# Eight weight pairs by seven products, and an order written by hand for all eight batches

## The chip, the cores and the metric

The kernel runs on one core of one Trainium2 chip. The metric is the device time of one execution in microseconds: 708.32 us is the median of the 3 runs before the change (706.35 to 708.89).

## The reference

Two softmax attentions per head, then a two-layer block on all 4608 tokens. Batch 8, 8 heads, 576 tokens, head width 64, 32 packed rows; model width 512, inner width 2048.

```python
def sm_attn(qq, kk, vv):
    a = softmax(qq @ kk.T / 8)          # over the last axis
    return a @ vv
p_packed = sm_attn(p, k, v)             # 32 rows per head
x = sm_attn(q, p_packed, p_packed)      # 576 rows per head, heads side by side: 4608 x 512
h = x @ w_in                            # 512 -> 2048
g = h * clip(h + 3, 0, 6) / 6
out = g @ w_out                         # 2048 -> 512
```

q, k, v and p are float32; w_in and w_out come as float64 and are narrowed on the chip.

## The kernel before, in words

**Precision.** The large products are made from float32r parts: each operand is split into a high and a low part, and each product is three matmuls (high·high, high·low, low·high; `product`, from L967).

**First layer.** The values of the second attention are folded into w_in: `u_m` multiplies the packed rows of a batch with each quarter of w_in into `m_hi`, `m_lo` (matmuls at L350), so that `first_product` (L929) makes one of 16 blocks f of h, transposed, from the attention weights `a_hi`, `a_lo` by six matmuls, three for each of two groups of heads. A block covers 256 or 320 tokens of one half of a batch, c = 0 or 1; `ps_h` holds two blocks.

**Gate.** `gate_into` writes min(relu(h+3), 6)·h with ScalarE (L940) and VectorE (L941). A block's last 64 columns of the wide half are edge rows, put aside in `bnd` by GpSimd (L965), and two batches' edges make a block of 128 rows.

**Second layer.** For a single block f, `gated` splits 256 columns into parts (ScalarE L946, VectorE L947), and `single_product` adds 2 x 3 matmuls of 512 columns (L969) to two banks. Two blocks 2i, 2i+1 can be taken as a pair: the 2x2 product of token halves and weight quarters is made by **seven** products of 256 columns, 21 matmuls (`pair_product`), from sums of the gated values (VectorE L1241, L1249, L1254) that GpSimd splits (L947, in `parted`). The weight side, T1 to T4, is made once, in batch 1, by `combine` (POOL L1072, VectorE from L1083 on); T3 takes the place of a quarter of w_out, and T1, T2, T4 lie in one of four slots. Batch 1's second half uses four pairs (`FIRST_PAIRS`), each half of batches 2 to 7 six pairs (`PAIRS = 6`) and four single blocks after them. Pairs 4 and 5 share slots with 0 and 1: `t_kept` in DRAM holds them, and `fetch_t` (L1105) brings two back per half.

**End of a half.** After the last pair `pair_product` reads the four banks A to D: one ScalarE copy of C (L1134), a GpSimd add (L1136) and three VectorE adds of D (L1139). The four single blocks then go on into A and B, two VectorE adds (L1153) finish the rows, and SyncE stores them (L1156). The edges of batches 4 to 7 are made by pairs in `moe_edges`, those of 2 and 3 inside batch 3, those of 0 and 1 by single products in batch 1.

**Attention of the next batch** runs beside the second layer: scores in two rounds of 288 columns (`scores`, `both_halves`), whose PSUM banks are `ps_a` and, where both go at once, two accumulator banks.

**Batch 0** has its own path: `first_attention` with transposed loads, `s2` whose scores lie head by token and are turned by VectorE (L852), scaled on GpSimd (L866) and turned back (L868), then `first_moe` over whole blocks (L607).

**Order.** Batch 0 is in the order of `PLAN`, one word for each step of a generator (611 words). It fixes PE, ACT, DVE, POOL and SP, SP being the queue on which nearly all transfers are asked for. Its loads go k, rest of k, two blocks of w_out (`lo0 lo2`), v of the first four heads, q, then w_in among the rest. From batch 1 on, no order is written: `fill` calls parts of the next attention at fixed steps (`STAGES`, `LATE`, `TURN`, `FETCHES`), and the framework's scheduler puts them among the loop's own instructions.

Of the kernel before, what the change touches and what calls it, by code (L numbers as in the profile page):

```python
# [25 lines left out]
TURN = (
    (5, 5, 6, 6, 7, 7, 7), (7, 8, 8, 9, 9, 9, 10), (10, 10, 11, 11, 12, 12, 12), (13, 13, 13, 14, 14, 15, 15),  # L30
    (27, 27, 28, 28, 28, 29, 29), (29, 29, 30, 30, 30, 31, 31),
)
# [2 lines left out]
PLAN = """
in in in in lo0 lo2 in in k0 in p li0 k1 in p k0 k2 k1 kr k2 in s0 kr b2 s0 b0 k3 s0 b2 li1 s0 warm b2 s0 in
k3 b2 in b0 s1 s0 li2 q1 b2 e0 q1 c0 s1 b2 e0 q0 c0 li3 s0 s1 v0 q0 s0 s1 s1 v0 b0 lp s1 b0 e1 a0 v0 c1 qr
v0 e1 c1 s1 a0 z0 qr b0 s1 a0 z0 b0 v1 a0 z0a a1 z0a upper a1 z0a lo1 q2 v1 li4 a1 q3 q2 z0a a1 v1 q3 v1 z0a  # L40
z1 z1 li7 a2 m0 z1a a2 m1 a2 z1a a2 lo3 a3 z1b z0a lk0 a3 z1b z1b z0a z1b z0a z1a z0a z1b lo5 z1a b1 li6 z1a
z1b m0 z1b b1 z1a z1a z1b z0a a4 z1a m0 li5 z1b z0a warm a3 z1b z0a m1 m0 z1b a7 lk2 z1a h0 m0 z1a m1 b1 a7
z1a b1 b3 h0 b3 lo4 b3 a3 warm r0 m1 a4 r0 b3 m2 lo8 tp h1 r0 m1 a7 y0 b1 h1 r0 m2 lo6 a4 x0 b1 r1 a4 x0 m2
m2 a6 r1 x0 a6 m2 h2 a7 tk0 r1 h2 y1 a5 lk3 r1 a5 x0 y1 a5 x1 r2 a6 a5 b5 x1 r2 b3 x1 tk2 r2 y0 h3 a6 b4 r2
lk1 h3 b4 b5 m4 x1 b3 r3 b4 li8 b5 m4 b4 li10 r3 x2 li9 m4 m4 x2 lo7 r3 m4 b5 below h4 b4 tk3 y3 b6 h4 b4 y3
lq1 y2 b6 x2 r3 b5 x2 b6 r4 tk1 x3 b6 b8 r4 x3 a8 b5 S a8 x3 a8 r4 y4 a8 S S S S x3 b8 y4 h5 a10 li11 r4 a10
lo9 h5 a10 a9 b8 lq3 x4 b8 r5 x4 b6 r5 S x4 y2 a10 r5 tq1 h6 lo10 b8 r5 lq2 h6 y5 a9 y5 S x4 a9 r6 b8 x5 a9
S b7 S x5 r6 a11 x5 li12 S a11 a11 h7 b6 r6 a11 S h7 r6 x5 b9 r7 li13 m8 S lv b7 b7 x6 r7 y6 b7 m8 x6 y7 r7
# [125 lines left out]

# [1338 lines left out]
```

## Time and profile before

| what | value |
|---|---|
| median of 3 runs | 708.32 us (706.35 to 708.89) |
| the profiled execution's own time | 709.52 us |
| its span, first to last instruction | 707.7 us |
| mean granted TensorE clock | 0.99 |
| PE, DVE, ACT, POOL busy | 97%, 77%, 61%, 47% of the span |
| moved by DMA | 111.15 MB, mean 157 GB/s |
| critical chain by engine | PE 82%, DVE 7%, DMA 5%, issue 2% |

The span leaves out what lies around the program, 1.8 us here. A PE shown as busy is one whose modelled matmuls overlap, so the pitch from one start to the next, not the duration, tells what a matmul costs in a row of them.

### The profile page before, as it was taken

What the parts mean: (1) busy time and instruction counts of PE and PEld (TensorE: products, weight loads), DVE (VectorE), ACT (ScalarE), POOL (GpSimd) and SP (SyncE); (2) the same over time, 40 slices, a digit from 0 to 9 for tenths busy, and PEclk for the clock granted to TensorE, in tenths of its full rate; (3) what the DMA queues carried; (4) which work ended last, traced back from release to release, by engine and by line L of the source; (5) the groups of instructions that cost most, each with busy time, mean ns of one, the idle gap of its engine ahead of it and who ended that gap; (6) DMA issues with size and microseconds to landing.
All of it is one profiled execution on the core that took longest, in us unless ns stands there. A gap on an engine that the chain in (4) does not pass through costs nothing.

```text
span 707.7 us, 16190 instructions
## 1 busy us (share of the span) xinstructions
PE 684.7 (97%) x5924; PEld 591.9 (84%) x5924; DVE 544.2 (77%) x1227; ACT 428.8 (61%) x1004; POOL 335.9 (47%) x515
## 2 busy tenths in 40 slices
PE   6599999999999999999999999999999999999997
PEld 4477877888879888899898888899888988899997
DVE  2897788788999759877788777877698778867754
ACT  5798876556566646565455655656475755565553
POOL 2475541113425456371272626474453646475552
PEclk9699999999999999999999999999999999999999
DMA  9989852955338655465554647375755644340330
GB/s 277 310 216 240 218 141 88 287 150 116 117 123 208 161 131 210 127 158 108 107 200 125 164 103 232 121 158 129 196 200 143 168 127 150 129 170 1 120 119 30
DMA packets 199679, 111.15 MB, mean 157 GB/s; under 512 B 173489, under 2 KB 185265, under 8 KB 195761
## 3 DMA queue, kind: packets, MB, share of 16 engines
q1 hardware_dynamic: 199056, 109.94, 55.8%
q8 instruction: 46, 0.75, 0.4%
q14 instruction: 33, 0.26, 0.1%
q10 hardware_dynamic: 544, 0.20, 0.1%
HBM read 92.27 MB, written 17.83 MB: 156 GB/s over the span
## 4 chain that ended last, share of the span: by engine, by line
PE 82%; DVE 7%; DMA 5%; issue 2%; SPq 1%; ACT 1%; POOL 1%; DVEq 0%; ACTq 0%; POOLq 0%
PE acc L969 48%; PE ps_hh L929 22%; PE ps L350 5%; PE ps_h L607 3%; DMA w_again<-w_kept 2%; PE ps L470 1%; SPq L294 1%; DMA room<-in_q_dram 1%; PE ps L440 1%; DMA wt<-t_kept 1%; DVE tr L555 1%; DMA p_nat<-in_p_dram 1%; DVE osb L1153 1%; PE ps L273 1%; DVE t L941 0%
## 5 line engine op out<-in xcount | busy, mean ns | idle before, releaser
L929 PE MATMUL ps_hh<-a_hi,m_hi 128*128 128x320 f32 (+1 forms) x448 | 133.5, 298 | 1.0 <-DVE t L941 0.9
L929 PE MATMUL ps_hh<-a_lo,m_hi 128*128 128x320 f32 (+1 forms) x448 | 133.0, 297 | 0.0
L929 PE MATMUL ps_hh<-a_hi,m_lo 128*128 128x320 f32 (+1 forms) x448 | 132.7, 296 | 0.0
L969 PE MATMUL acc<-wo_hi,g 128*128 128x512 f32 x304 | 109.0, 402 | 0.0
L940 ACT ACTIVATE t<-ps_hh,three 128x320 f32<-128x320 f32 (+1 forms) x148 | 73.5, 500 | 47.4 <-PE ps_hh L929 36.0
L941 DVE SCALAR_TENSOR_TENSOR t<-t,ps_hh 128x320 f32<-128x320 f32 (+1 forms) x148 | 65.7, 445 | 45.1 <-ACT t L940 44.4
L947 POOL TENSOR_TENSOR ge<-t,ge 128x256 fp32r<-128x256 f32 x76 | 60.3, 793 | 80.8 <-ACT ge L946 32.1
L929 PEld LDWEIGHTS ps_hh<-a_hi,m_hi 128*128 128x128 f32 x448 | 84.7, 189 | 7.7 <-DVE t L941 2.7
L929 PEld LDWEIGHTS ps_hh<-a_lo,m_hi 128*128 128x128 f32 x448 | 84.7, 189 | 4.8 <-issue 1.9
L929 PEld LDWEIGHTS ps_hh<-a_hi,m_lo 128*128 128x128 f32 x448 | 84.7, 189 | 1.7 <-issue 1.3
L965 POOL COPY bnd<-t 128x64 f32<-128x64 f32 x76 | 24.2, 318 | 120.0 <-DVE t L941 117.8
L969 PE MATMUL acc<-wt,ga 128*128 128x256 f32 x492 | 80.4, 284 | 0.3 <-ACT ga L946 0.2
L969 PE MATMUL acc<-wo_hi,ge 128*128 128x256 f32 x328 | 77.8, 285 | 0.0
L947 POOL TENSOR_TENSOR gf<-tb,gf 128x256 fp32r<-128x256 f32 x76 | 65.0, 855 | 17.5 <-ACT gf L946 14.9
L947 POOL TENSOR_TENSOR ga<-t,ga 128x256 fp32r<-128x256 f32 x76 | 60.8, 800 | 24.4 <-ACT ga L946 24.2
L969 PEld LDWEIGHTS acc<-wo_hi,g 128*128 128x128 f32 x304 | 56.1, 188 | 16.2 <-issue 3.0
L969 PEld LDWEIGHTS acc<-wt,ga 128*128 128x128 f32 x492 | 68.0, 190 | 1.2 <-issue 0.5
L969 PEld LDWEIGHTS acc<-wo_hi,ge 128*128 128x128 f32 x328 | 57.5, 190 | 7.0 <-issue 2.8
L969 PE MATMUL acc<-wo_lo,g 128*128 128x512 f32 x152 | 60.1, 395 | 0.0
L555 DVE STREAM_TRANSPOSE tr<-nat 128x576 f32<-128x576 f32 x56 | 42.4, 765 | 16.7 <-DMA nat<-in_q_dram 10.4
L940 ACT ACTIVATE tb<-ps_hh,three 128x256 f32<-128x256 f32 (+1 forms) x76 | 37.9, 499 | 23.0 <-PE ps_hh L929 18.6
L969 PE MATMUL acc<-wt,gf 128*128 128x256 f32 x246 | 50.1, 283 | 0.3 <-DMA wt<-t_kept 0.3
(234 smaller groups left out, 1780.5 us busy)
## 6 DMA issues: line engine op xcount, KB each, us to landing
w_again<-w_kept SPq DMA_DIRECT2D x24, 1024.0 KB, 4.8
wt<-t_kept SPq DMA_DIRECT2D x26, 768.0 KB, 5.2
out_dram<-osb SPq DMA_DIRECT2D x35, 256.0 KB, 2.4
nat<-in_k_dram SPq DMA_DIRECT2D x112, 72.0 KB, 3.2
nat<-in_q_dram SPq DMA_DIRECT2D x112, 72.0 KB, 2.7
raw_out<-in_moe_w_out_dram SPq DMA_DIRECT2D x10, 512.0 KB, 5.1
raw_in<-in_moe_w_in_dram SPq DMA_DIRECT2D x10, 512.0 KB, 5.6
w_kept<-w_in_sb SPq DMA_DIRECT2D x4, 1024.0 KB, 7.6
```

Of the source, the lines that this page charges most:

```text
L273: nc.tensor.matmul(banks[x][NPK * a:NPK * a + NPK, :n * P], state["pp"][half, NPAIR * x + a], cols[half, :, a], start=True, stop=True,)
L294: nc.sync.dma_start(out=t[r:r + 32], in_=src[b, 2 * a + h, :, 32 * c:32 * c + 32].rearrange("(t i) j -> i t j", i=32),)
L350: nc.tensor.matmul(pair[x][NPK * a:NPK * a + NPK, :n], rows[half, a], c, start=True, stop=True)
L440: nc.tensor.transpose(out=pair[x][:, c * P:(c + 1) * P], in_=e[x][:, c * P:(c + 1) * P], identity=ident)
L555: nc.vector.transpose(out=t, in_=state.pop(("nat", which, b, a)))
L607: nc.tensor.matmul(h[:, hf, :HS], mm[:, g, fs], aa[:, hf * HS:(hf + 1) * HS], start=(g == 0 and i == 0), stop=(g == NG - 1 and i == 2),)
L929: state["first"] = nc.tensor.matmul(h[:, :n], mm[:, g, fs], aa[:, t0:t0 + n], start=(g == 0 and i == 0), stop=(g == NG - 1 and i == 2),)
L940: state["relu"] = nc.scalar.activation(out=t[:, :n], in_=h, func=AF.Relu, bias=three)
L941: state["gate"] = nc.vector.scalar_tensor_tensor(out=t[:, :n], in0=t[:, :n], scalar=6.0, in1=h, op0=ALU.min, op1=ALU.mult)
L947: engine.tensor_sub(out=lo, in0=x, in1=hi.bitcast(F32))
L965: nc.gpsimd.tensor_copy(out=bnd[:, f, side * REM:side * REM + REM], in_=t[:, boff:boff + REM])
L969: nc.tensor.matmul(out, lhs[x], rhs[y], start=first and i == 0, stop=last and i == 2, skip_group_check=True)
```

## The change

- `PAIRS` is 8 and each half of batches 2 to 7 has pairs alone, in the order `ORDER` or, reversed in use, `DOWN`. `SLOT` gives pairs 0 to 5 and 7 four slots; pair 6's parts lie in the room of the first 12 edge blocks. Three fetches per half replace two.
- Edge rows of batches 2 to 6 go to DRAM (`e_kept`), two blocks at a time, and come back in batch 7: the edges of 2 to 5 by pairs (`edge_half`), those of 6 and 7 by `last_edges`.
- Scores go in one round of 512 and 64 columns; the 64 lie in the banks of `ps_h`.
- Batch 0's second attention has tokens on the partitions: the scores come out so from the matmul, the weights are scaled on VectorE, and PE turns them.
- Batch 0's loads are steps of their own, and q and v stand ahead of w_out and of all but one block of w_in.
- `PLANS` holds eight orders, one word for each instruction or small group, for all engines and batches (some 4,700 words); `fill` and its tables are gone.

```diff
-PAIRS = 6
+PAIRS = 8
 FIRST_PAIRS = 4
-FETCHES = (((5, 1), (7, 0)), ((5, 4), (7, 5)))
+ORDER = (1, 0, 2, 3, 5, 4, 6, 7)
+DOWN = (5, 4, 3, 7, 6, 1, 0, 2)
+SLOT = {0: 0, 1: 1, 2: 2, 3: 3, 4: 0, 5: 1, 7: 2}
+KEPT = {0: 0, 1: 1, 2: 2, 4: 3, 5: 4, 7: 5}
-    "zm00": "P", "zm10": "P", "al10": "D", "zm19": "P",
+    "zm00": "D", "zm10": "D", "al10": "D", "zm19": "D",
...
+PLANS = (
+    """
+lp0 lk_0 k0 p k1 lk_1 lkr p lqr k2 k2 k0 k1 s0 lq_1 kr k3 k3 kr s0 li0 warm s1 s1 s0 a0 s0 s0 s0 lq_2 lq_0 q1 s1
+e0 c0 s1 s1 c0 q0 q1 s0 lv_0 e0 v0 s0 s1 s1 e1 v0 lv_1 s1 q0 v0 lq_3 a0 c1 c1 qr qr a0 v0 z0 z0 z0a a0 li1 li3
...
+f00 'e17 'e19 nlk2 'c1d nlk3 'c1d 'a1e 'b1f 'x1d 'x1d 'nZ f00 'x1b f01 'o01 'e1e 'o00 'b1f 'g1d g00 g00 g00 'd1d
...
+g02 'x1f b01 'x1f 'x1d 'x1f a00 M3 'd1f b01 'r1 g02 g01 f03 g03 M3 'x1d c01 d01 g03 'r1 a02 b03 'r1 'r1 e03 'r1
+'e1d 'x1f 'o10 M3 f04 e00 f04 f05 g03 x01 'e1f b03 d01 f05 g05 'o11 x01 g03 x01 g05 c01 x03 x01 x01 a02 e02 x03
...
+def written(ch):
+    for b, plan in enumerate(PLANS):
+        for name in plan.split():
+            near = {"'": b - 1, '"': b + 1}.get(name[0])
+            yield (b, name) if near is None else (near, name[1:])
...
     def spare_pair():
         if steady:
-            return [spare_ps(x) for x in range(2)]
+            return [ps_h.tile([P, 512], F32, name="ps_s", tag="h") for _ in range(2)]
...
+    def all_rows(b, lhs, rhs):
+        cuts = (slice(0, HS), slice(HS, S)) if b == 1 else (slice(0, NB), slice(NB, S))
...
         def s2(g, halves):
-            parts = products(s, g, made["pp"].rearrange("p (x h) n -> p x h n", x=2), qt, lambda: rows["qr"])
+            for y in range(2):
+                for h in range(4):
+                    for x in range(2):
+                        half = slice(64 * x, 64 * x + 64)
+                        o = y * P + NPK * h
+                        nc.tensor.matmul(
+                            s[:, x, o:o + NPK], qt[2 * g + h // 2][half, h % 2, y], pp[half, g, h], start=True, stop=True
+                        )
...
-            for o in range(cols.start, cols.stop, HS):
-                nc.vector.transpose(out=flat[:, o:o + HS], in_=s[:, o // HS])
...
-            nc.vector.transpose(out=at[:, cols], in_=flat[:, cols])
+            for x in range(n):
+                for y in range(2):
+                    nc.tensor.transpose(out=at[x][:, y * P:(y + 1) * P], in_=z4[:, x, 4 * y:4 * y + 4]..., identity=ident)
+            for x in range(n):
+                nc.vector.transpose(out=at[x][:, 2 * P:HS], in_=z4[:, x, T // 2 - 1])
...
     def keep_edge(b, keep, f, boff, side):
+        nc.gpsimd.tensor_copy(out=place, in_=keep["t"][:, boff:boff + REM])
+        if 1 < b < LAST and f % 2:
+            nc.sync.dma_start(out=e_kept[b // 2, :, two, cols], in_=stage8()[:, f % 8 - 1:f % 8 + 1])
...
+        def summed():
+            nc.scalar.activation(out=r1, in_=bank("C"), func=AF.Copy, scale=sixth)
+            (nc.vector if end else nc.gpsimd).tensor_tensor(out=u1, in0=r1[:, :H2], in1=r1[:, H2:], op=ALU.add)
+            added(r1[:, H2:], 0, u1)
+            added(r2[:, :H2], 1, u1)
+            added(r2[:, H2:], 0, r2[:, :H2])
...
     with tc.manual_schedule(engines=HAND):
-        for name in PLAN.split():
+        for b, name in written(ch):
...
+            else:
+                next(ch[b, name])
```

In the words, f, g, a to d, x stand for the first product, the gate, the four splits and the seven products of a step (c, then the step in hexadecimal); r for the adds at the end of a half, o for its stores; n with S, E, V, T, Z, M for the next batch's attention; a mark ' for the batch before, " for the one after.

## Rows read from the trace of the kernel before

**Rows 1.** Section 1 of the profile's page: busy time and share of the span.
```profile
PE 684.7 (97%) x5924; PEld 591.9 (84%) x5924; DVE 544.2 (77%) x1227; ACT 428.8 (61%) x1004; POOL 335.9 (47%) x515
```

**Rows 2.** Busy time by stretch of the span: start and end, length, then busy us and (x instructions) of PE, PEld, DVE, ACT and POOL, the granted clock, the DMA share and GB/s. The first stretch is batch 0's attention, the second its layers, from 116 on come batches 1 to 7.
```profile
0.00:38.80 38.80, 23.01 (x343) 16.25 (x343) 21.76 (x57) 25.71 (x55) 16.23 (x20) 0.82 1.03 289
38.80:116.00 77.20, 76.77 (x596) 60.95 (x593) 64.31 (x124) 62.38 (x113) 38.14 (x38) 1.00 0.69 176
116.00:200.00 84.00, 82.85 (x637) 67.64 (x636) 70.40 (x170) 49.89 (x119) 23.41 (x41) 1.00 0.58 160
200.00:280.00 80.00, 79.51 (x712) 69.21 (x711) 65.67 (x155) 47.84 (x117) 38.82 (x60) 1.00 0.64 176
360.00:440.00 80.00, 79.49 (x732) 69.98 (x732) 62.85 (x139) 46.33 (x115) 39.89 (x60) 1.00 0.57 154
```

**Rows 3.** Waits of PE alone, over the whole span: who waited, for whom, us in total, times, longest.
```profile
PE ps_t L886 <- DVE m_lo L286: 5.3, 1, 5.3
PE ps_w L803 <- issue: 2.0, 1, 2.0
PE ps_hh L929 <- DVE t L941: 0.9, 2, 0.5
PE ps L350 <- DMA w_again<-w_kept: 0.8, 1, 0.8
PE acc L969 <- ACT ga L946: 0.7, 2, 0.5
PE ps_h L607 <- DVE t L1308: 0.4, 1, 0.4
PE acc L969 <- DMA wt<-t_kept: 0.3, 1, 0.3
```

**Rows 4.** The chain that ended last, in order of time (start us, us, what): two blocks of the first layer at 256 columns, one pair's seven products, one single block's product, and one round of 512 columns of the small matmuls.
```profile
405.69 1.44 PE ps_hh L929 x12
407.13 2.52 PE acc L969 x21
136.25 1.39 PE acc L969 x6
375.50 1.10 PE ps L350 x16
```

**Rows 5.** The timeline of PE: one round of 288 columns of scores.
```profile
403.58 0.71 PE L350 MATMUL ps<-tr,p_tr 64*32 64x288 f32 x16
```

**Rows 6.** Groups of instructions by line and shape: count, busy us, mean ns of one, idle time before them. The product of a pair with T4, three matmuls each, then the splits and sums of pairs and, fifth, the split of a single block.
```profile
L969 PE MATMUL acc<-wt,gf 128*128 128x256 f32 x246 | 50.1, 283 | 0.3 <-DMA wt<-t_kept 0.3
L947 POOL TENSOR_TENSOR ge<-t,ge 128x256 fp32r<-128x256 f32 x76 | 60.3, 793 | 80.8 <-ACT ge L946 32.1 <-issue 16.7 <-POOL bnd L965 12.9
L947 POOL TENSOR_TENSOR gf<-tb,gf 128x256 fp32r<-128x256 f32 x76 | 65.0, 855 | 17.5 <-ACT gf L946 14.9 <-POOL ge L947 1.1 <-POOL bnd L965 0.8
L947 POOL TENSOR_TENSOR ga<-t,ga 128x256 fp32r<-128x256 f32 x76 | 60.8, 800 | 24.4 <-ACT ga L946 24.2 <-issue 0.2
L947 DVE TENSOR_TENSOR g<-t,g 128x256 fp32r<-128x256 f32 x72 | 30.1, 423 | 6.4 <-ACT g L946 4.7 <-PE acc L969 0.5
L947 POOL TENSOR_TENSOR ga<-tb,ga 128x128 fp32r<-128x128 f32 x76 | 37.4, 492 | 3.3 <-ACT ga L946 2.8 <-PE acc L969 0.6
L1241 DVE TENSOR_TENSOR t<-t 128x128 f32<-128x128 f32 x76 | 24.6, 323 | 1.9
L1249 DVE TENSOR_TENSOR t<-t,tb 128x256 f32<-128x256 f32 x76 | 43.5, 572 | 1.5
L1254 DVE TENSOR_TENSOR tb<-tb,t 128x128 f32<-128x128 f32 x76 | 36.8, 484 | 1.6
```

**Rows 7.** The chain that ended last, first 45 us.
```profile
5.21 8.16 DMA room<-in_q_dram
35.27 1.41 POOL x_out L203
36.67 1.45 POOL w_in_sb L203
```

**Rows 8.** Groups by line and shape in the first 38.8 us: VectorE's turns of the scores, and GpSimd's scaling.
```profile
L852 DVE STREAM_TRANSPOSE z<-ps_w 128x288 f32<-128x288 f32 x4 | 1.8, 466 | 1.5 <-PE ps_w L731 1.5
L866 POOL TENSOR_TENSOR z<-z,den 128x288 f32<-128x288 f32 x2 | 1.3, 672 | 0.4 <-DVE den L862 0.4
L866 POOL TENSOR_TENSOR z<-z,den 128x576 f32<-128x576 f32 x1 | 1.2, 1239 | 1.3 <-DVE den L864 1.3
```

**Rows 9.** Groups by line and shape: what reads the banks at the end of a half.
```profile
L1134 ACT ACTIVATE osb<-acc 128x512 f32<-128x512 f32 x14 | 8.4, 597 | 2.1 <-PE acc L969 2.0
L1136 POOL TENSOR_TENSOR osb<-osb 128x256 f32<-128x256 f32 x14 | 10.8, 772 | 24.7 <-ACT osb L1134 24.7
L1139 DVE SCALAR_TENSOR_TENSOR osb<-acc,osb 128x256 f32<-128x256 f32 x42 | 16.3, 415 | 4.8 <-POOL osb L1136 4.8
```

**Rows 10.** The timeline of the last microseconds.
```profile
703.22 1.39 DVE L1153 SCALAR_TENSOR_TENSOR osb<-acc,osb 128x512 f32<-128x512 f32 x2 [1.62 <-PE acc L969]
703.48 0.39 PE L969 MATMUL acc<-wo_hi,g 128*128 128x512 f32 x1
```

**Rows 11.** Section 6 of the page: a fetch of a slot, KB, median us from issue to landing.
```profile
wt<-t_kept SPq DMA_DIRECT2D x26, 768.0 KB, 5.2
```

More of the change, by code (lines that the diff above doesn't have):

```diff
@@ L44 @@
[L44 to L48, printed above, removed]
@@ L836, in s2 @@
             state["a", 0, g] = (hi, lo)
[L837 to L839 removed]
+            n = 2 // halves
+            made["z", g] = [(s, z, mx, den, hi, lo, slice(i, i + n)) for i in range(0, 2, n)]
             yield
         def s2_part(g, i):
[L843 to L845 removed]
@@ L1047, in packed_attention_moe @@
-    FOUR = B - 4
-    blocks, slots = {}, {}
+    blocks, slots, parked = {}, {}, {}
+    LAST = B - 1
     def block(i, name):
@@ L1109, in sums_of @@
+    def sums_of(ch, b, c, pairs, singles, rows):
         banks, made = {}, {}
+        end = (b, c) == (LAST, 1)
         def bank(x):
@@ L1127, in pair_product @@
                     bank(x)[:, half * H2:half * H2 + H2], lhs[l], block(i, r), fresh,
-                    i == pairs[-1] and x in "CD",
+                    i == pairs[-1] and (x in "CD" or not singles),
                 )
-            if i == pairs[-1]:
-                sixth = 1.0 / 6.0
-                r1, r2 = (gp.tile([P, DM], F32, name="osb") for _ in range(2))
-                made["r"] = r1, r2
-                nc.scalar.activation(out=r1, in_=bank("C"), func=AF.Copy, scale=sixth)
-                u1 = r2[:, H2:]
-                nc.gpsimd.tensor_tensor(out=u1, in0=r1[:, :H2], in1=r1[:, H2:], op=ALU.add)
-                def added(dst, half, other):
+                yield
@@ new lines, in single_products, with finished @@
+        def single_products(f, keep):
+            g = keep["g"]
+            for k, x in enumerate("AB"):
+                second_product(
+                    f, bank(x), g[:, k * P:(k + 1) * P], g[:, (2 + k) * P:(3 + k) * P],
+                    first=False, last=f == singles[-1],
+                )
+                yield
+        def finished(k):
+            r = made["r"][k]
+            for cut in ((slice(0, H2), slice(H2, DM)), (slice(H2, DM), slice(0, H2)))[k] if end else (slice(0, DM),):
+                own = cut if k == 0 or singles else slice(cut.start, min(cut.stop, H2))
+                if own.start < own.stop:
@@ L1193, in down @@
-    def down(b, c):
-        return c == 0 or b == FOUR + 3
-    def moe_pairs(b, c, fill):
-        pairs = list(range(FIRST_PAIRS if b == 1 else PAIRS))
-        if down(b, c):
-            pairs.reverse()
-        n_pairs = len(pairs)
-        steps = [2 * i + k for i in pairs for k in range(2)] + list(range(2 * n_pairs, NF))
+                        out=r[:, own], in0=bank("AB"[k])[:, own], scalar=1.0 / 6.0, in1=r[:, own], op0=ALU.mult, op1=ALU.add
+                    )
+                    yield
@@ L1204, in moe_pairs, with pairs_half @@
+                nc.sync.dma_start(out=rows[k][:, cut], in_=r[:, cut])
+                yield
+        ch[b, f"r{c}"] = summed()
+        for k in range(2):
+            ch[b, f"o{c}{k}"] = finished(k)
+        return pair_products, single_products
+    def pairs_half(ch, b, c):
+        pairs, steps = steps_of(b, c)
         even = b % 2 == 0
```

1118 lines of the change are left out of this document (645 added, 473 removed), and 4 rows, old and new, of the table ENGINES.

## The prediction

> **What bounds the kernel now.** I read the page's busy shares first, then the busy time by stretch, then PE's own waits, then the chain that ended last. PE is busy for 97% of the span, VectorE for 77%, GpSimd for 47% [rows 1]. By stretch, PE is short only in the first 38.8 us, with 23.0 us busy at a mean granted clock of 0.82; in the stretches shown after that it is idle for 0.4 to 1.2 us in some 80, at full clock [rows 2]. PE's waits say the same: the long ones, 5.3 and 2.0 us, lie in batch 0's attention, and the waits shown for gates, splits and transfers of the layers (0.9, 0.8, 0.7, 0.4, 0.3) come to 3.1 us together [rows 3]. So the kernel is 39 us of start, some 665 us in which PE has work without a break, and 3.8 us of end: the last matmul ends at 703.48 + 0.39 = 703.9 in a span of 707.7 [rows 10]. Only four things can move the time: fewer PE columns, an earlier start, new waits of PE, and the end.
>
> All sums stand on the profiled execution, 709.5 us (span 707.7 and 1.8 around it). It is 1.2 us above the median of the three runs, 708.3; I take that off at the end.
>
> **Products.** A pair costs PE 21 matmuls of 256 columns, 2.52 us in the chain or 0.120 us each; a single block's step costs 6 of 512 columns in 1.39 us, 0.232 each [rows 4]. Two single blocks are thus 2.78 us and a pair 2.52. Before, there are 246 / 3 = 82 pairs [rows 6]: 4 in batch 1, 12 halves of 6, and 6 for the edges. After, there are 4 + 12 x 8 + 8 = 108. That is 26 x 12 = 312 fewer wide matmuls and 26 x 21 = 546 more narrow ones; the one edge block still made by sums has two pairs more, which trades 6 wide for 12 narrow. In all 318 x 0.232 = 73.8 us go and 558 x 0.120 = 67.0 come: **-6.8 us**, all on the path, since nothing else holds PE there.
>
> [...]
>
> **Scores in one round.** Sixteen small matmuls take 0.71 us at 288 columns and 1.10 at 512 [rows 4, 5], so 1.7 ns for each column more; two rounds of 288 cost 1.42, one of 512 and one of 64 cost 1.10 + 0.33. Nothing changes on PE. The 64 columns now lie in the first layer's two banks; their short reads are covered by the products of pairs that PE has in hand, and without that cover each of some 12 would cost about one copy, 0.4 us (single-block split, [rows 6]). I take 0.
>
> **Work that moves off PE's path.** A pair needs on GpSimd 0.793 + 0.855 + 0.800 + 0.492 = 2.94 us of splits, on VectorE 0.323 + 0.572 + 0.484 = 1.38 us of sums in place of two splits of 0.423 [rows 6]: 26 more pairs add 76 us to GpSimd (336 to 412) and 14 us to VectorE. Two more weight combinations, eleven operations each at the nearest shape's 0.42, add 9. VectorE goes from 77% to about 81%, GpSimd to 59%. Both are covered by PE while their work comes early enough; the rival below says what it costs when not.
>
> **Transfers.** Each half fetches three slots instead of two, a fetch landing 5.2 us after its issue [rows 11]. In both orders a fetched pair stands at least four places behind the one whose slot it takes, so three whole pairs of 2.52 + 1.44 us [rows 4], 12 us, cover it. Eight small stores of edges a batch join SyncE's queue; behind them stand next loads, not PE. I take 0; if the cover fails, each costs what such waits cost now, 0.3 to 0.8 us [rows 3].
>
> **The start.** The chain waits for q until 5.21 + 8.16 = 13.4 us [rows 7]. Two blocks of w_out, 1.05 MB, were asked for ahead of it; at 289 GB/s [rows 2] that is 3.6 us, now behind q and v. w_out comes later by that much, and its narrowing must then share VectorE, ScalarE and GpSimd with the second softmax; its first use is after the first gate. At the other end of the stretch the chain runs through GpSimd narrowing weights (1.41 and 1.45 us, [rows 7]), after GpSimd had scaled the softmax for 1.24 + 2 x 0.67 = 2.6 us [rows 8]. Those 2.6 go to VectorE, which loses four turns of 0.466 [rows 8] and gives the turning back to an idle PE. Bounds: nothing if narrowing still ends last (the last wait of the start is 1.1 us for a narrowed w_in block, [rows 3]); 3.6 + 2.6 = 6.2 if both add. They lie one after the other on partly the same chain, so I take a little over half, **-3.5**.
>
> **Waits.** The 3.1 us of steady waits can go at best, or stay; I take **-1.5**.
>
> **Ends of halves.** Today four single blocks, 4 x 1.39 = 5.6 us, run between the last pair and the next half, and hide the reading of the banks: 0.60 on ScalarE, 0.77 on GpSimd, three adds of 0.415 on VectorE, 2.6 us [rows 9]. After, the next half's first pair wants banks C and D with no single blocks before it. Between the last product into C and the next half's first into D, the written order puts first-layer half-blocks and remaining products: counting these at 0.36 to 0.44 and 0.36 us I get 1.7 to 3.5 us at ten ends, where some also have a quarter product of 1.1. At 2.6 for the chain, about 3 us are exposed in all, less the quarter products: **+2**, bounds 0 and 9 (0.75 at each of 12 ends).
>
> **The very end.** Now the last singles hide the reading too. After, the chain ScalarE 0.60, add about 0.43, three adds and three finishing ones of 0.415 [rows 9] is 3.5 us from the last product into C, with 0.7 us of PE products still beside it, then the store. That leaves 2.8 us of arithmetic after the last matmul where two adds took 1.39 [rows 10]: **+1.5**, bounds 0 and 2.
>
> **Sum.** 709.5 - 6.8 - 3.5 - 1.5 + 2 + 1.5 = 701.2; on the scale of the median 700.0.
>
> **Rival 1: VectorE and GpSimd decide, gain mostly lost.** From 200 to 280 us VectorE is already busy for 65.7 of 80 [rows 2], and the two extra combinations and pairs fall there and just before. VectorE sums of 128 columns take 0.323 in one place and 0.484 in the other [rows 6], so they do meet delay beside GpSimd's splits, and GpSimd's work grows by a quarter. Against it: even with 11 us more, 116 to 280 us holds 147 of 164. If such delay costs PE 0.45 us in each of 12 halves (one of today's two waits for a gate, [rows 3]), 5.4 us come back: **705**. [...]
>
> **Rival 2, slower: the banks at the ends of halves.** Place: first products into C and D of a new half. VectorE's three adds stand in its queue behind gates and softmax steps, so the 2.6 us can stretch. At 1.5 us exposed at each of 12 ends, 18 in place of 2, the time is **716**. It decides from 10.3 / 12 = 0.86 us an end; by 1.16 the kernel is measurably slower. For it: there are no single blocks left as cover. Against: the order interleaves the old half's last products with the new half's first blocks.
>
> **Rival 3: the start doesn't move** because narrowing still ends last: 700.0 + 3.5 = **703.5**, still faster; it lies inside the forecast's range.
>
> **How the numbers follow.** Forecast with rival 3 inside: 0.74; rival 1: 0.17; rival 2: 0.09. A change of 0.5%, 3.5 us, is about what a measurement of this kernel can tell: faster is below 704.8, slower above 711.9. Of the forecast 0.70 falls below; rival 1 straddles the line, 0.07 faster and 0.10 same; 0.04 of the forecast is same; rival 2 is slower. Faster 0.77, same 0.14, slower 0.09. Range: the good ends of start and waits with no exposed ends give 709.5 - 6.8 - 6.2 - 3.1 + 1 - 1.2 = 693, and the products' pitch may come out nearer the shorter one: 690. Upward it takes in rival 1 with its start unmoved: 708.
>
> **What the changed profile would show.** Right: 324 matmuls with T4, no single blocks after 280 us before the last edges, PE's dense part beginning at about 35 us, PE waits of a few tenths at the ends of halves, and VectorE near 81%. Wrong: PE waits above 1 us for the bank reads, VectorE at 95% in 116 to 280 us with PE waiting for gates, a dense part still starting at 38.8, or PE waiting for slot fetches.

## The result, and the profile after

The changed kernel takes **718.18 us** (median of 6 runs, 716.16 to 723.0); the kernel before, run beside it, 708.61 (706.35 to 710.53). The ratio is 1.0147 with a 95% interval of 1.0126 to 1.0168: slower by 1.5%, where I had said 700 us and 0.77 for faster. The profiled execution took 718.5 us, its span 716.4, so 8.7 more than before.

Section 1 of the page after the change, answering [rows 1]:

```profile
PE 687.6 (96%) x6200; PEld 607.6 (85%) x6200; DVE 554.4 (77%) x1282; ACT 433.9 (61%) x1062; POOL 391.4 (55%) x616
```

PE has more matmuls and about the same busy time, and VectorE's share has not moved. The stretches of [rows 2] after the change:

```profile
0.00:38.80 38.80, 28.41 (x378) 21.39 (x378) 18.46 (x51) 20.64 (x46) 8.17 (x13) 0.78 0.88 272
38.80:116.00 77.20, 75.69 (x584) 59.09 (x585) 69.01 (x127) 67.27 (x121) 42.90 (x39) 1.00 0.89 226
200.00:280.00 80.00, 76.90 (x697) 67.58 (x696) 65.35 (x166) 46.20 (x121) 41.24 (x66) 0.98 0.64 182
360.00:440.00 80.00, 79.70 (x774) 72.63 (x773) 63.51 (x151) 48.36 (x127) 50.10 (x81) 1.00 0.69 184
```

From 360 to 440 PE runs as it did before; from 200 to 280 it is idle for 3.1 us, where it was idle for 0.5. In the first 38.8 us it is busier by 5.4 us and yet not further on. PE's waits after the change, answering [rows 3]:

```profile
PE ps L487 <- DMA w_again<-w_kept: 4.9, 3, 2.5
PE ps_t L969 <- DVE z L964: 3.3, 1, 3.3
PE acc L1028 <- DVE osb L1301: 1.6, 2, 1.3
PE ps_hh L1137 <- DVE t L1151: 1.3, 3, 0.5
PE acc L1028 <- DMA wt<-t_kept: 1.0, 1, 1.0
PE acc L1028 <- POOL ge L1159: 0.7, 1, 0.7
```

The longest wait of the layers is now for a transfer, `w_again`, the refetch of a quarter of w_in. The same by half, worked out from the starts of PE's matmuls (a half's length runs to the first matmul of the next, idle is the sum of PE's pauses over 0.1 us; lengths of batches 3 and 7 also differ because edge products moved from one to the other):

| stretch | before: length, idle | after: length, idle |
|---|---|---|
| to the first matmul of the first layer | 33.40 | 34.90 |
| batch 0 behind it | 85.84, 1.54 | 84.22, 1.56 |
| batch 2, second half | 41.52, 0.00 | 51.89, 5.18 |
| batch 3, second half | 50.25, 0.00 | 41.79, 0.97 |
| batch 7, second half | 55.66, 0.00 | 68.04, 2.94 |
| all idle behind the start | 4.45 | 12.42 |
| last matmul to the end of the span | 3.85 | 5.88 |

In sum: there are 558 matmuls of 256 columns more and 318 of 512 fewer, -6.8 us at the pitches of [rows 4]; the start costs +1.5, the very end +2.0, and the distances between the large matmuls beyond their pitch (where over 0.1 us) grew from 15.5 to 27.7, +12.2, of which 8.0 is idle. That is +8.9 against the measured 8.7. More than half of the 12.2 (0.6 before, 7.7 after) lies in one half of batch 2.

This is one profile of each kernel, and parts that no edit touched move by a microsecond or two. In the eight profiles whose batch 0 is that of the changed kernel, the first layer starts at 32.6 to 34.9 us and batch 1 at 118.7 to 121.8 (before the change, one profile: 33.4 and 119.2). In the seven whose second half of batch 2 has the changed kernel's order, that half takes 50.0 to 52.8. So the +1.5 of the start is not firm, and the long half is.

That half's SyncE queue, in order of time (start us, us of the issues, what, count):

```profile
258.05 2.11 SPq L453 DMA_DIRECT2D p_nat<-in_p_dram  x4
267.44 0.34 SPq L1668 DMA_DIRECT2D w_again<-w_kept  x1
267.89 0.39 SPq L1182 DMA_DIRECT2D e_kept<-stage  x1
268.32 4.14 SPq L433 DMA_DIRECT2D nat<-in_k_dram  x4
272.57 0.45 SPq L1182 DMA_DIRECT2D e_kept<-stage  x1
273.06 2.31 SPq L1111 DMA_DIRECT2D wt<-t_kept  x2
275.47 0.38 SPq L1668 DMA_DIRECT2D w_again<-w_kept  x1
```

The queue stands from 260 to 267.4 because the refetch waits until nM2, the matmuls that read the one buffer of w_in, are done; the next batch's k and two weight fetches stand behind it. nM1 then wants the refetched quarter at 270.2 and gets it at 272.7; nM0 waits 2.1 us more, M3 0.3. The two long waits differ in kind. The refetch for nM1 was asked for late and landed 5.1 us later, near the median of 5.3 (4.8 before). The one for nM0, asked for at 275.5, landed 9.0 us later, behind the requests that the queue had held back: DMA lay idle before the refetch and was full after it (share and GB/s, the last two columns).

```profile
264.00:266.00 2.00, 2.00 (x25) 1.29 (x9) 2.00 (x5) 0.59 (x4) 2.00 (x4) 1.00 0.00 0
278.00:280.00 2.00, 2.00 (x19) 2.00 (x18) 1.43 (x5) 1.51 (x3) 0.24 (x1) 1.00 1.03 410
```

The changed kernel moves 126.16 MB in all, 15 more than before; what that alone costs was not tried. And the wait has a second price, read from the granted clock (seventh column from the left pair on: PE, PEld, DVE, ACT, POOL, then clock, DMA share, GB/s):

```profile
272.00:274.00 2.00, 1.31 (x16) 0.22 (x17) 0.03 (x1) 0.00 (x0) 1.30 (x2) 0.84 1.16 188
274.00:276.00 2.00, 2.00 (x13) 2.00 (x9) 1.27 (x3) 0.96 (x3) 0.47 (x1) 0.50 0.81 240
276.00:278.00 2.00, 2.00 (x15) 2.00 (x14) 1.08 (x2) 0.83 (x3) 0.83 (x2) 0.80 0.99 341
```

PE had been idle for 2.5 us and had then run 16 small matmuls; the granted clock then stood at 0.50 from 273.4 to 276.8, where matmuls of 320 columns start 0.27 us apart in place of 0.15. By estimate, half of some 3 us of full work, that is worth 1.5 us.

### The profile page after: what moved, and what is told of

The parts are those of the page before. It is cut to its first block, busy times and chain, and to the rows that moved or that the text cites. A ratio compares the mean times of both kernels' runs of the same rounds, so it can differ in the third digit from the quotient of the medians.

```text
span 716.4 us, 17077 instructions
## 1 busy us (share of the span) xinstructions
PE 687.6 (96%) x6200; PEld 607.6 (85%) x6200; DVE 554.4 (77%) x1282; ACT 433.9 (61%) x1062; POOL 391.4 (55%) x616
## 2 busy tenths in 40 slices
DMA packets 215556, 126.16 MB, mean 176 GB/s; under 512 B 186800, under 2 KB 199088, under 8 KB 211760
## 4 chain that ended last, share of the span: by engine, by line
PE 75%; DVE 11%; DMA 5%; ACT 3%; POOL 2%; issue 2%; SPq 1%; DVEq 0%; ACTq 0%; POOLq 0%
PE acc L1028 41%; PE ps_hh L1137 20%; PE ps L487 5%; PE ps_h L687 4%; DMA w_again<-w_kept 3%; PE ps L600 1%; DVE t L1151 1%; PE ps_w L919 1%; POOL ga L1159 1%; DVE osb L1301 1%; PE ps L570 1%; DMA wt<-t_kept 1%; DVE tr L677 1%; DVE wt L1079 1%; DVE g L1159 1%
## 5 line engine op out<-in xcount | busy, mean ns | idle before, releaser
L1159 POOL TENSOR_TENSOR ga<-t,ga 128x256 fp32r<-128x256 f32 x100 | 79.6, 796 | 59.7 <-ACT ga L1157 53.3
L1028 PE MATMUL acc<-wo_hi,ge 128*128 128x256 f32 x432 | 106.0, 285 | 1.6 <-POOL ge L1159 0.7
L1028 PE MATMUL acc<-wt,ga 128*128 128x256 f32 x648 | 102.8, 284 | 0.5 <-POOL ga L1159 0.4
L1028 PEld LDWEIGHTS acc<-wt,ga 128*128 128x128 f32 x648 | 88.7, 190 | 5.1 <-issue 4.2
L1151 DVE SCALAR_TENSOR_TENSOR t<-t,ps_hh 128x320 f32<-128x320 f32 (+1 forms) x124 | 55.6, 449 | 37.9 <-ACT t L1149 37.1
L1028 PEld LDWEIGHTS acc<-wo_hi,ge 128*128 128x128 f32 x432 | 78.6, 189 | 6.4 <-DVE osb L1301 1.8
L1149 ACT ACTIVATE tb<-ps_hh,three 128x256 f32<-128x256 f32 (+1 forms) x100 | 49.9, 499 | 40.9 <-PE ps_hh L1137 17.8
L1151 DVE SCALAR_TENSOR_TENSOR tb<-tb,ps_hh 128x256 f32<-128x256 f32 (+1 forms) x100 | 44.5, 447 | 37.5 <-ACT tb L1149 36.7
L1157 ACT CAST ga<-t 128x256 fp32r<-128x256 f32 x100 | 40.4, 405 | 36.4 <-PE acc L1028 21.6
L1028 PE MATMUL acc<-wo_lo,ge 128*128 128x256 f32 x216 | 60.5, 280 | 0.0
L1159 POOL TENSOR_TENSOR ga<-tb,ga 128x128 fp32r<-128x128 f32 x100 | 49.7, 498 | 19.1 <-ACT ga L1157 17.8
L1157 ACT CAST ge<-t 128x256 fp32r<-128x256 f32 x100 | 40.4, 404 | 28.3 <-DVE t L1357 24.0
```

The lines of the kernel that those rows point to most:

```text
L1028: nc.tensor.matmul(out, lhs[x], rhs[y], start=first and i == 0, stop=last and i == 2, skip_group_check=True)
L1149: nc.scalar.activation(out=t[:, :n], in_=h, func=AF.Relu, bias=three)
L1151: nc.vector.scalar_tensor_tensor(out=t[:, :n], in0=t[:, :n], scalar=6.0, in1=h, op0=ALU.min, op1=ALU.mult)
L1157: nc.scalar.copy(out=hi, in_=x)
L1159: engine.tensor_sub(out=lo, in0=x, in1=hi.bitcast(F32))
```

## Experiments

Two questions: what makes the 12 us between matmuls, and why the start gave nothing. **Theory A** says that single places do it, first the refetch; **theory B** is the prediction's rival 1, VectorE and GpSimd set the pace; **theory C** came up on the way: the order in SyncE's queue. The times of one variant spread by 1 to 8 us; the length of a half is read from the one profile of each. In the orders below, nM2, nM1 and nM0 are the parts of the next batch's `u_m` that read a quarter of w_in each from one buffer, w1 and w0 the refetches into that buffer, ft15 the fetch of pair 5 in a batch's second half, nlk0 a load of the next batch's k.

### Batch 2: spacing of the refetch

```diff
-x13 x13 nM2 nM1 e13 d15 ... x17 f1a nZ x15 nZ ... x19 x19 d17 ft14 ... "ntp g1b w0
+x13 x13 nM2 e13 d15 ... x17 f1a nZ x15 nM1 nZ ... x19 x19 d17 w0 ft14 ... "ntp g1b
```

nM0 moved likewise, M3 into batch 3.

> The changed kernel with one thing different: in batch 2 the refetched blocks of w_in are read later (nM1 by some 2.8 us of matmuls, nM0 by some 2.8, M3 behind the next half's first block), and the second refetch is asked for ahead of a fetch of weight combinations. Nothing is left out. Theory A (the loss sits at a few places, and the largest is the single buffer through which w_in is refetched): the three waits for it, 2.64 + 2.28 + 0.43 us, go to under 0.7 together, the clock that fell to half behind the first of them stays at full (1.5 us more), so -5.5 to -7 us against the changed kernel's 718.2: 711 to 713, ratio to before 1.004 to 1.007. Theory B (VectorE and GpSimd set the pace with eight pairs): what the refetch gives back is taken by waits for splits and gates a little later: -2 at most, 716 to 718.

Measured (e1): 721.20 us, ratio 1.0181 (1.0146 to 1.0216). Theory A fails as a whole: the half became only 2.7 us shorter (49.23). The granted clock was 0.989 in the mean of the kernel (0.984 in the changed kernel) and the wait for w_in fell to 1.0 us, but PE now waited 1.7 us for a weight fetch and 0.8 and 1.1 us for gates. Behind the first late transfer stood others.

### Batch 2: the fetches first

> The changed kernel with SyncE's written order mended: each fetch of weight combinations is asked for as soon as the pair before it in its slot has been read (in all halves), and in batch 2 nM1 is read some 4.2 us of products later and its successor's refetch asked for at once. Nothing is left out. In the spacing experiment the waits for w_in fell (7.7 to 1.2 us at the refetches), but a fetched combination then came 1.9 us late and gates 0.6 and 1.2 us late. Theory C (the queue of SyncE: a refetch that waits, loads and stores stand ahead of the fetches): waits on transfers fall to under 0.7 us in all, in batches 2 and 3 together -8 against the changed kernel, some 1.5 of gates come in their place: 711 to 712.5. Theory B (VectorE and GpSimd set the pace there): transfers no longer wait, but gates and splits take over for 4 us and more: 715 to 718.

Measured (e5): 750.75 us, ratio 1.0601. Here the fetch of pair 1 in batch 2 stands ahead of the store of pair 5, which shares its slot, so that later halves multiply by other weights; the instructions are the same. It is no like-for-like comparison, but shows how this queue can be ordered too early: SyncE stood 109.4 us for PE's reads of slots (60.9 in the changed kernel), and loads that others needed stood behind. Waits of SyncE's queue in this kernel, then of PE:

```profile
SPq L1112 <- PE acc L1029: 109.4, 29, 9.8
```
```profile
PE ps_hh L1138 <- DVE t L1152: 13.4, 7, 4.4
PE ps L488 <- DMA w_again<-w_kept: 10.2, 3, 6.4
```

The same order with the scaling back on GpSimd:

> The order of the fetches mended as in the experiment of that name, and the scaling of batch 0's second softmax given back to GpSimd (where the first layer started 1.6 us earlier, in one profile, than in the changed kernel). Nothing is left out. If both count and add: 709.5 to 711. If only the fetches count: 711 to 712.5. Theory B: 714 to 718.

It (e8) measured 751.39, with the same fetch ahead of its store, and says nothing more.

### Batch 2: three fetches first, by hand

```diff
-... x15 w1 nM2 g18 ... x13 x13 nM2 nM1 ... "ntk0 ft15 d17 ... ft14
+... x15 ft15 w1 nM2 g18 ... x13 x13 ft14 nM2 ... "ntk0 d17 ... x19 x19 nM1 d17 w0
```

> The changed kernel with three fetches of weight combinations moved in SyncE's written order, by hand and only where a wait was seen: in batch 2 ft15 ahead of the refetch w1 and ft14 behind the last product of the pair it replaces, in batch 3 ft00 ahead of a store; and nM1 of batch 2 read 4.2 us of products later. Nothing is left out. (Asking for every fetch at the first possible moment held the loads behind it and made 33 us of waits.) Theory C, the order of SyncE's queue: in batches 2 and 3 waits on transfers fall from 6.5 to under 1 us, the half clock behind them goes, gates take 1.5 us: 711 to 713. Theory B, VectorE and GpSimd set the pace there: 715 to 718.

Measured (e10): 721.94, ratio 1.0194 (1.0168 to 1.0219). No transfer was late for PE, and still the half took 52.69 us, with 5.0 us in one piece. VectorE's and SyncE's timelines show why:

```profile
277.20 0.78 DVE L677 STREAM_TRANSPOSE tr<-nat 128x576 f32<-128x576 f32 x1 [5.74 <-DMA nat<-in_k_dram]
```
```profile
266.88 0.34 SPq L1668 DMA_DIRECT2D w_again<-w_kept  x1
269.68 0.32 SPq L1111 DMA_DIRECT2D wt<-t_kept  x1
271.07 4.20 SPq L433 DMA_DIRECT2D nat<-in_k_dram  x4
```

The next batch's k is asked for at 271.07 to 275.27, so VectorE stands at the turn of it for 5.7 us, and the gate that PE needs is behind that turn in VectorE's written order: its VectorE part starts at 280.14, after the turn (277.20) and three instructions more, and PE at 280.68. In the changed kernel the same turn had waited 2.7 us, unseen, since PE was waiting for w_in then.

With the scaling and the end edited as well:

> The previous experiment's kernel with two more edits: the scaling of batch 0's second softmax back on GpSimd, and the last pair of the whole kernel with C and D ahead of the second product into B. Nothing is left out. The end alone is worth 0.7 us (5.9 to 5.2 from the last matmul), the scaling 0 to 1.6: 709 to 711.5, so 0.7 to 2.3 below the previous experiment, and still above the 708.3 of before, since the scores of the second softmax stay.

Measured (e11): 723.88 us; the half was again 51.8 us long.

### Batch 2: k first, the gate before the copy, nM0 later

```diff
-... x15 w1 nM2 g18 ... x13 x13 nM2 nM1 ... e18 "nlk0 ...
+... x15 ft15 "nlk0 w1 nM2 g18 ... x13 x13 ft14 nM2 ... e18 ...
```

> The changed kernel with batch 2's order on SyncE's queue mended once more: ft15 and the next batch's first k load ahead of the refetch w1, which waits there for its buffer, ft14 behind the last product of the pair it replaces, w0 as soon as nM1 is read, nM1 4.2 us of products later. Nothing is left out. With the fetches alone moved ahead, VectorE waited 5.7 us for that k load, 5.0 of them passed on to TensorE. Theory C (the order of SyncE's queue, with whatever stands last in it): no wait above 0.6 us is left in batch 2's second half, its length goes from 51.9 to 45.5 us or less, 711 to 713. Theory B (VectorE and GpSimd set the pace there): the length stays above 48.5, 715 or more.

Measured (e13): 718.68 us, ratio 1.0136. The half: 49.10, 2.8 shorter, with one wait of 2.3 us left, for a gate behind the copy of nM1 in ScalarE's order. The time is that of the changed kernel all the same: in this profile batch 0 behind the start, which the edit does not touch, took 85.7 us instead of 84.2. Next, ScalarE's order was turned round, with nM1 1.1 us earlier:

> The changed kernel with batch 2's order as in the experiment on the k load, but nM1 1.1 us of products earlier and its copies and subtractions behind the gates of the next block on ScalarE and VectorE. Nothing is left out. Theory C (orders only): batch 2's second half has no wait above 0.6 us and is 46 to 47 us long, where it was 51.9 in the changed kernel and 49.1 in that experiment; 714 to 716. Theory B: it stays at 48.5 or above, 717 to 719.

Measured (e15): 718.76 us, ratio 1.0142. The half: 49.11; that wait is gone, and nM0 waits 2.4 us for its quarter. Last, nM0 later:

> e15 with nM0 of batch 2 read 2.8 us of products later, and the last pair of the whole kernel with C and D ahead of the second product into B. Nothing is left out. Theory C (orders only): no wait above 0.6 us in batch 2's second half, which is 46 to 47 us long (51.9 in the changed kernel, 49.1 in e15), 5.2 us from the last matmul to the end: 714.5 to 716.5. Theory B: some other wait of 1.5 us or more takes the place of nM0's and the half stays above 48.5: 717.5 to 719.

Measured (e18): 715.69 us, ratio 1.0120 (1.0085 to 1.0154), some 0.7 of it expected from the end; the interval overlaps that of the changed kernel, so the times alone show no gain. In the profile the span is 713.8 and the half 48.33, below the 50.0 to 52.8 of the kernels whose batch 2 is unedited. PE has no wait for w_in left in the whole kernel and one of 0.3 us for a weight fetch; in this half two gates are late, 1.5 and 1.1 us. VectorE ahead of the first of them:

```profile
278.69 0.75 DVE L654 TENSOR_TENSOR a_lo<-at,a_hi 128x576 fp32r<-128x576 f32 x1
279.36 0.69 DVE L669 TENSOR_TENSOR m_lo<-ps,m_hi 128x512 fp32r<-128x512 f32 x1
279.96 0.74 DVE L632 TENSOR_REDUCE mx<-z 128x18 f32<-128x576 f32 x1
280.74 0.80 DVE L634 TENSOR_TENSOR z<-z,mx 128x576 f32<-128x576 f32 x1
281.46 0.47 DVE L1151 SCALAR_TENSOR_TENSOR t<-t,ps_hh 128x320 f32<-128x320 f32 x1
```

It works without a break, and the gate, whose ScalarE part was done at 280.8, stands 0.7 us behind a softmax step. That ScalarE part itself had begun 0.5 us late, at 280.27, held by a split of GpSimd until 280.24. The second gate stood on ScalarE behind a copy of m_hi; its VectorE part followed at once. So C accounts for 3.6 us of this half's excess. What is left there, some 2.6 us, are waits behind orders of ScalarE, VectorE and GpSimd; none of these runs takes load off VectorE or GpSimd there, so whether order or load makes them, theory B, is not shown. Whether a better order of all queues would bring the half to the 45 us that its matmuls take wasn't tried.

### The ends of halves

```diff
+            if i == pairs[-1] and c < 2 and (b, c) not in ((2, 1), (4, 0), (6, 0)):
+                order = [order[n] for n in (2, 3, 0, 5, 4, 1, 6)]
```

> The changed kernel with the seven products of the last pair of a half in another order (C and D before the second product into B), in ten of thirteen halves and at the very end, so that C is finished two products of 0.36 us earlier and can be read earlier. Nothing is left out. Theory A (the bank reads at the ends are exposed): the waits for them, some 3 us in all now, fall by 1 to 2, and the time from the last matmul to the end of the span, 5.9 us, by 0.7: 715.5 to 716.5, ratio 1.010 to 1.012. Theory B (late splits and gates hold the first pair of the next half, not the banks): no change beyond 0.5 us.

Measured (e2): 721.44, ratio 1.0174. The end did what was expected (5.16 us from the last matmul), the halves did not: the waits for banks went from 1.6 to 1.3 us, while others for gates grew from 1.3 to 2.6.

### The start

> The changed kernel with the first two blocks of w_out asked for ahead of q and v, as before the change. Nothing is left out. My forecast: 1.05 MB ahead of q make the chain of the start 3 to 3.6 us later: 721 to 722. Rival: the start ends with the narrowing of weights; earlier weights then give time back where q comes later, and the time stays within 1 us of 718.2, or falls by up to 1.5 us.

```diff
-... lkr p lqr k2 k2 k0 k1 s0 lq_1 ... z0a z0a v1 v1 lo0 lo1 z0a
+... lkr p lqr k2 k2 k0 k1 s0 lo0 lo1 lq_1 ... z0a z0a v1 v1 z0a
```

Measured (e4): 723.11, ratio 1.0207 (1.0166 to 1.0248); first layer at 36.98, 2.1 later where I had said 3 to 3.6. The rest of the 4.9 lies behind the start; in this profile the second half of batch 4 alone is 3.9 us longer. So inside the changed kernel the load order is worth some 2 us of start. What, then, costs as much again? The chain of the start after the change:

```profile
17.95 1.91 PE ps_w L919 x32
24.64 3.63 PE ps_w L919 x32
33.31 0.69 PE ps_t L969 x2
35.25 2.89 PE ps_h L687 x12
```

The scores with tokens on the partitions are 64 matmuls of 32 columns, 5.5 us. In the chain of the start before, the scores of 256 columns that they replace took 1.7:

```profile
18.63 0.59 PE ps_w L720 x16
25.25 1.08 PE ps_w L720 x13
```

Twice as many of the new ones:

> The changed kernel with each of the 64 matmuls of 32 columns that make the scores of batch 0's second softmax issued twice into the same place. Nothing is left out. They take 1.9 us in the first group of heads and 3.6 in the second, and I did not count them. If they are on the path that sets the start (theory: they took what the earlier loads gave), the first layer starts 5 to 5.5 us later and the time rises by as much: 723 to 724. Rival: the start ends with the narrowing of weights, whatever the scores do: first layer up to 2 us later, time within 1 us of 718.2.

```diff
+                        for _ in range(2):
                             nc.tensor.matmul(s[:, x, o:o + NPK], qt[...], pp[half, g, h], start=True, stop=True)
```

Measured (e6): 725.78, ratio 1.0252 (1.0227 to 1.0276); first layer at 38.97, 4.1 later. They are on the path to the first layer. The converse:

> The changed kernel with batch 0's second softmax as before the change: scores in 32 matmuls of 256 and 32 columns with the packed rows on the partitions, turned by VectorE, scaled on GpSimd. All else, the load order too, is as after the change. Nothing is left out. Doubling the narrow matmuls moved the first layer by 4.1 us and the time by 7.6. If they are what took the gain of the start, the first layer starts 3 to 4.5 us earlier than in the changed kernel (30.5 to 32), and the time is 712.5 to 715. Rival: the start ends with the narrowing of weights: first layer at 33.5 or later, 717 to 718.5.

Measured (e12): 724.99, ratio 1.0220, against both expectations. The first layer did start at 30.34, 4.6 us earlier, but its second block at 43.7, as in the changed kernel (43.8; before 42.6). The chain in between:

```profile
32.13 1.19 POOL z L955
33.32 1.22 POOL w_in_sb L353
34.76 1.00 POOL a_lo L961
38.27 3.25 PE ps_h L687 x12
```

GpSimd's scaling, narrowing and subtraction end last there, and PE, shown as busy for 5.2 us of the 12 from 24 to 36, runs the 12 matmuls at a granted clock of 0.50 (36 to 40 us, 0.56 in the mean of 40 to 44): 3.25 us, where the changed kernel's 12 at 44.00, at 1.00, take 1.66. The rest of the loss lies in batches 2 to 4, where transfers landed later (waits of 2.6, 3.3 and 1.3 us); the landing of a refetch was 4.7 to 10.1 us in this profile, 4.7 to 9.0 in the changed kernel's and 4.6 to 7.2 before. That orders with little room scatter more for it is likely, and not shown. With VectorE scaling:

> e15 with batch 0's second softmax as before the change, its scaling on VectorE as after it, and the end's last pair with C and D first. Nothing is left out. If GpSimd's chain (scaling 1.2, narrowing 1.2, subtraction 1.0 us) held the second block of the first layer, that block starts 1 to 2 us earlier than in the changed kernel (42 to 43 us against 43.8), and with the end's 0.7 this is 1.7 to 2.7 below e15. If VectorE, which is busy without a gap from 28 to 36 us, takes its place: 43.5 or later, and 0.7 below e15.

Measured (e16): 724.04, the second block at 46.4: VectorE took GpSimd's place, with a 4.2 us wait for its `a_lo`. All three edits together:

> The two edits of e12 and e13 together, and at the very end the last pair with C and D ahead of the second product into B. Nothing is left out. If they add: -4 (softmax), -6 (batch 2), -0.7 (end) against 718.2: 706 to 709, level with the 708.5 of before; below it only if the batch 0 behind the start shortens as well. If the start's gain is lost in batch 0's weights: 710 to 712.

Measured (e14): 722.58; the gains do not add in the time. The first layer starts at 30.2 and the half of batch 2 takes 49.1, as in the single edits, but batch 0 behind the start takes 89.8 (84.2 in the changed kernel) and the first half of batch 4 38.3 (34.5). The scaling by itself, both ways:

> The changed kernel with the scaling of batch 0's second softmax given back to GpSimd, three instructions. Nothing is left out. My forecast gave the move of the scaling to VectorE a share of the start's gain (2.6 us of GpSimd ahead of its narrowing). If that holds, the first layer starts 1 to 2.6 us later here: 719 to 721. If the start ends on VectorE and ScalarE, which are busy for nearly all of 32 to 45 us, the move gained nothing and giving it back costs at most the longer instructions, 2 x 0.2 us: 717.5 to 718.7.

Measured (e3): 719.69, ratio 1.0164 (1.0132 to 1.0196): no difference from the changed kernel that the times show, though the first layer starts at 33.29; batch 1 starts at 119.0, as in the changed kernel (119.1).

```diff
-    "zm00": "P", "zm10": "P", "zm19": "P"
+    "zm00": "D", "zm10": "D", "zm19": "D"
```

> The kernel before with only this part of the change: the scaling of batch 0's second softmax on VectorE. Nothing is left out. My forecast had GpSimd's 2.6 us of scaling ahead of the narrowing that ends the start; if so the second block of the first layer's rows starts 1 to 2.6 us earlier than its 38.8 us, 706 to 707.5 against 708.5. If VectorE's chain sets the start, the scaling's 3 instructions of about 0.5 to 0.8 us there make it later: 709 to 710.5.

Measured (e17): 710.09 against 708.7, ratio 1.0021 (1.0006 to 1.0035): moving the scaling to VectorE is no gain but a small loss. The load order by itself:

> The kernel before with only this part of the change: the first two blocks of w_out are asked for behind q and v, and their narrowing is placed some 30 places later in the written order. Nothing is left out. In the changed kernel undoing this order cost 2.1 us of start and some 4.9 us in all; by my forecast's term the load order is worth -3 to -3.6 by itself: first layer at 30 to 31 us instead of 33.4, 704.5 to 706 against 708.3. Rival: the start ends with the narrowing of weights: first layer 0 to 1 us earlier, 707.5 to 709.

Measured (e9): 716.63, ratio 1.0110 (1.0092 to 1.0129), first layer at 40.9. I had put the narrowing of w_out too early for its later load: ScalarE, and PE behind it, did nothing for 4 us (PE, PEld, DVE, ACT, POOL, clock):

```profile
16.00:20.00 4.00, 0.00 (x0) 0.00 (x0) 0.33 (x1) 0.00 (x0) 0.00 (x0) 0.99 1.05 386
```

So this run shows what a late load at the head of ScalarE's written order did, and not what the order is worth. Last, the half clock:

> The changed kernel with 22 more matmuls of 256 columns on zeros in batch 0's attention, 6 ahead of the second group's scores, 16 in the 3 us in which TensorE waits for the second softmax. Nothing is left out. In the changed kernel the granted clock is at half from 21 to 37.6 us, and before the change from 22.9 to 35.7. If the half clock sets part of the start, the second group's scores take 1.9 instead of 3.6 us and the first 12 matmuls of the first layer 1.6 instead of 2.9: first layer 1 to 1.5 us earlier, batch 0's second block up to 2.5 us earlier, 715.5 to 717. If it does not, or the clock stays at half all the same, the time stays at 718.2 or rises by the 1.3 us of matmuls put on the path.

Measured (e7): 727.09, ratio 1.0265. The clock came up (0.68 from 24 to 28 us, 1.00 from 28 to 40), and the second group's scores and the first layer's start ran at 1.00:

```profile
23.41 4.30 PE L994 MATMUL ps_t<-pps 128*128 128x256 f32 x12
27.64 1.97 PE L919 MATMUL ps_w<-pp,rows 64*128 64x32 f32 x32
30.48 7.07 PE L994 MATMUL ps_t<-pps 128*128 128x256 f32 x32
```

1.97 us in place of 3.63. But the 6 and 16 added matmuls appear as 12 and 32 and took 4.3 and 7.1 us, most of it on the path, not the 1.3 that I had expected; the first layer started 4.0 later. Half clock is a real part of the start, and this is no way to buy it back.

## Why the prediction was wrong, point by point

- **Products, -6.8: right.** The counts differ by 558 and 318, as forecast, at the same pitch; a pair's 21 matmuls in the chain, and a first-layer pair beside it:

```profile
395.39 1.45 PE ps_hh L1137 x12
412.86 2.51 PE acc L1028 x21
```

The 21 stand 0.120 us apart, as before; no run shows the shorter pitch that took my range from 693 down to 690.

- **Scores in one round, 0: right.** The matmuls that the trace shows as `64*32` and `128*32`, each counted from its start to the next one's, take 59.1 us behind the start before and 58.9 after.
- **Transfers, "I take 0": the step that failed first.** I counted how many pairs lie between two users of a slot. What decides is when SyncE's queue comes to the request, and that stands in the written order with stores, loads and a refetch that waits for its buffer. The refetch of w_in, a wait of 0.8 in [rows 3], I didn't cost at all, though the written order sets its spacing anew. Refetch and slot fetches measure 4.9 + 1.0 us of waits in the changed kernel (0.8 + 0.3 before) and, by the estimate above, 1.5 of half clock; my price for a failed cover, 0.3 to 0.8, was taken from single waits of before, and the longest is now 2.5. In the half where most of it lies, another order took back 3.6 us (e18); no run shows that the time of the kernel comes back with it.
- **The start, -3.5: failed.** It measures +1.5, and over the eight profiles -0.8 to +1.5. The load order is worth -2.1 in the first layer's start (e4). The wait of 1.1 us on which I leaned for the lower bound is not among [rows 3]; it is in the trace, on GpSimd's narrowing of w_in (PE, at 38.2 us). "Gives the turning back to an idle PE" left out the 64 matmuls, 5.5 us in place of 1.7, half of them at a granted clock of 0.50, 3.63 us. And I added gains that lie on chains beside each other: undoing one part moved one chain and left the next (e12, e16, e3). Rival 3's outcome came, a start without gain, but hardly by its reason: up to the first layer the chain runs through scores, softmax and transposes more than through narrowing.
- **Waits, -1.5: failed.** The waits did not shrink: all idle behind the start went from 4.45 to 12.42 us, and PE's waits for the gates of the half-batches (0.9 in [rows 3]) are 1.3.
- **Ends of halves, +2: right in size, by luck.** Waits for banks come to some 2 us (1.6 in PE's waits above, 0.4 for the finishing adds), but 1.3 and 0.4 of them lie at the edges of batch 7; at the ends of halves, which the sum was about, one wait of 0.2 is left. Rival 2 did not come.
- **The very end, +1.5: nearly.** +2.0. ScalarE starts at 709.85, and the last adds, answering [rows 10]:

```profile
712.33 0.75 DVE L1327 SCALAR_TENSOR_TENSOR osb<-acc,osb 128x256 f32<-128x256 f32 x2
```
```profile
710.25 0.28 PE L1028 MATMUL acc<-wo_hi,ga 128*128 128x256 f32 x1
```

- **Rival 1, VectorE and GpSimd:** not in its form. VectorE stayed at 77%, and the three sums of a pair fell from 1.38 to 1.31 us, with 55 us of work added on GpSimd (I had said 76), answering [rows 6]:

```profile
L1357 DVE TENSOR_TENSOR t<-t 128x128 f32<-128x128 f32 x100 | 35.2, 353 | 1.2
L1372 DVE TENSOR_TENSOR t<-t,tb 128x256 f32<-128x256 f32 x100 | 50.8, 509 | 1.6
L1379 DVE TENSOR_TENSOR tb<-tb,t 128x128 f32<-128x128 f32 x100 | 44.5, 445 | 1.4
```

In the trace before, the sums of 128 columns that overlap no GpSimd instruction (24 of L1241, 8 of L1254) took 242 to 294 ns; those that lie beside GpSimd for over nine tenths of their time (35 and 58) took 356 and 516 in the mean, 845 at most. After, the first kind (48 of L1357, 26 of L1379) took 249 to 293, the second (32 of each) 447 and 543 in the mean, 846 at most. So single sums took longer beside GpSimd, but more of them met none, and over all sums the delay did not grow with GpSimd's work. What may be true of the rival is seen in e18: once transfers are in time, gates are next, behind the orders of ScalarE, VectorE and GpSimd.
- **The chances.** Slower had 0.09, all of it on rival 2. No case stood for the one resource that this change reorders for all eight batches, SyncE's queue.

What stays open: the waits are accounted for from the profiles, and no edit brought the time down clear of the scatter, so that the refetch and the queue cost the 9.6 us is in part argued. The 2.9 us of waits in batch 7's second half (1.3 for the bank of the last edges, 0.4 for finishing adds, 0.7 and 0.4 for splits) were not worked on, and no version here beats the kernel before.

## What to carry to other kernels

Where a change writes a new order for a queue that issues transfers, cost each request by when the queue reaches it, with every waiting request ahead of it, and look at each buffer that exists once; distance between users says only when it could be asked for. The stall of one queue can hide that of another: VectorE's 2.7 us at the turn of k did not show while PE waited for w_in, and 5.0 of its 5.7 us reached PE when that wait was gone (e10). So mend one wait and read the profile again before adding up gains. At a start where several chains end close to each other, work added to one showed (e6: 4.1 us later in the first layer, 7.6 in the time), and work taken from one did not come back in the time (e12, e16).
